# All contractions as pairs of 64-row passes, queries one head at a time inside the attention stream, on fixed bank pairs

## The chip, the cores and the metric

The kernel runs on one core of one Trainium2 chip. The metric is the device time of one execution in microseconds (us); lower is better.

The engines go by short names: PE is TensorE's matmuls and PEld its weight loads, ACT is ScalarE, DVE is VectorE, POOL is GpSimd and SPq is the queue of SyncE. The matmuls write into PSUM, which the program shares out as eight banks.

## The reference, cut to what matters

```python
# x [1,2048,448]; k, v caches [1,8,2048,256]; wq [448,4096]; wo [4096,448]; w_gate, w_up [448,1792]; w_down [1792,448]
xn = layernorm(x)
q  = (xn @ wq)                       # 16 heads of 256, two query heads share one k/v head
s  = softmax(q k^T / 16) v           # over the last 512 keys only
s  = s @ wo
g  = silu((gelu(xn @ w_gate) * (xn @ w_up)) @ w_down)
return x + s * g
```

The contractions are over 448 (queries, gate, up), 256 (scores), 512 (P V), 4096 (w_o) and 1792 (w_down). The rows are worked on in four chunks of 512, so the attention has 4 x 16 = 64 head steps, called "heads" below and numbered 0 to 63.

## The kernel before: the parts that matter

TensorE has 128 rows. A contraction of 448 = 3 x 128 + 64 does not fill it evenly, so the queries and gate/up are already computed as **pairs of 64-row passes**: two matmuls on the upper and the lower half of the rows, side by side, into two different PSUM banks. Phase 0 has the upper rows fill bank b and the lower rows bank b+1; phase 1 has it the other way round, so each bank ends with the full sum. The code makes phase 1 of a bank pair wait until its phase 0 has ended.

```python
def group(units, lo, hi, start, stop, phases=(0, 1)):
    for p in phases:
        ...
        for (b, w, wr, cols, reads, rreads, xts) in units:
            for k in ks:
                for u, j in ((0, ph), (1, 1 - ph)):          # rows 0-63, then rows 64-127
                    rows = slice(R * u, R * u + R)
                    lst.append((bank[b + j][:, lo:hi], l, xnT[rows, k, cols], ...))
            before = [last_row[b][0]] if b in last_row and last_row[b][1] != ph else []
            o = mms(lst, reads + rr + xb, b_ps[b:b + 2], before)
```

The other contractions are full 128-row passes. Queries come in blocks of 8 or 12 heads, then scores and P V alternate for as many heads. P V of a head follows its scores by two heads (LAG = 2), and alternates between two bank pairs (`m % 2 * 2`).

```python
def s_mm(m):                                             # scores of head m: 4 tiles of 128 rows
    for t4 in range(4):
        b = AB[t4]
        mms([(bank[b], qT[:, s, e, t4 * P:(t4 + 1) * P], kT[:, g, e, :], e == 0, e == 1) for e in range(2)], ...)
        # ACT: exp with row sum; DVE: reciprocal, then normalise into pn
        if t4 % 2 == 1:
            dma_t(pT..., pn...)                          # transposed by DMA

def pv(m):
    for e in range(2):
        b = BB[m % 2 * 2 + e]
        mms([(bank[b]..., va[:, g, j, e * P:(e + 1) * P], pT[:, x, :, :, j, :]..., j == 0, j == NJ - 1)
             for j in range(NJ)], ...)
        # e == 0: ACT copies the bank into oT; e == 1: DVE does

for m in range(NS):                                      # NS = 64
    if m in groups:                                      # 0, 8, 20, 32, 44, 56
        for i in range(m, groups[groups.index(m) + 1], 2):
            q_group(i, (cur, nxt)[i // 2 % 2])
    s_mm(m)
    ...
    if len(late) == LAG:
        pv(late.pop(0))
    ...                                                  # after each chunk: w_o, 4 tiles
```

`mms` issues a list of matmuls with one wait ahead and one semaphore at the end. Below, a "slot" is the time of one full pass or of one pair.

The softmax here doesn't subtract the row's maximum and nothing guards it: scores larger than these inputs give would overflow.

Of the kernel before, what the change touches and what calls it, by code (L numbers as in the profile page):

```python
# [164 lines left out]
def bass_recurrent_scan__sliding_block_cached__geglu_ffn__prompt_kernel(  # L165
# [34 lines left out]
    QS = 12  # L200

    es = ExitStack()
    with es:
# [86 lines left out]
        NPT, NPN, NP32 = 3, 3, 3  # L290
        pT, a, at = place("pT", [P, NPT, 2, 2, NJ, P], BF16, at=rf)
        b_pT = [sbuf_bufs(a + i * QC * NJ * 2, QC * NJ, 2) for i in range(NPT)]
# [7 lines left out]
        qT, a, at = place("qT", [P, QS, 2, QC], BF16, at=b_gl[0].lo - (QS - HG) * 2 * QC * 2)  # L300
        assert b_oT[-1].hi <= a
        b_qT = [[K.buf(a + (h * 2 + e) * QC * 2, QC * 2) for e in range(2)] for h in range(QS)]

# [136 lines left out]

        def warm(n, b, w):
            def fn(e):
                ins = None
                for i in range(n):
                    ins = e.matmul(bank[b][:, 0:w], lhsT=gl[:, 0, 0:P], rhs=gl[:, 0, 0:w], start=True, stop=True)
                return ins
            last_row[b] = (K.op("pe", fn, (b_gl[0],), b_ps[b:b + 2]), None)
# [48 lines left out]

        def down(c, pairs):
            for t4 in range(4):
                t = c * 4 + t4
                b = bk(pairs, t4)  # L500
                mms([(bank[b][:, 0:D], actT[:, c % 2, f, t4 * P:(t4 + 1) * P], wd[:, f, :], f == 0, f == NF - 1)
                     for f in range(NF)], [b_wd] + b_actT[c % 2], (b_ps[b],))
                s = t % 2
                act(tmp[:, s, :], bank[b][:, 0:D], ACT.Tanh, (b_ps[b],), b_tmp[s], scale=0.5)
                K.op("dve", lambda e, t=t, b=b, s=s: e.scalar_tensor_tensor(
                    out=g2[:, t, :], in0=tmp[:, s, :], scalar=1.0, in1=bank[b][:, 0:D],
                    op0=ALU.add, op1=ALU.mult), b_tmp[s] + [b_ps[b]], (b_g2[t],))
# [29 lines left out]
        warm(2, 2, QC // 2)  # L537
# [82 lines left out]
        def q_group(n, pairs):  # L620

            c, h = divmod(n, Hq)
            units = [(b, lambda j, k, i=i: wq[:, k, (h + i) * Dh + j * P:(h + i) * Dh + (j + 1) * P],
                      wqr[:, h + i, :], slice(c * QC, (c + 1) * QC), b_wql[h // HG][:1], b_wql[h // HG][1:], b_xnT[c * 4:c * 4 + 4])
                     for i, b in enumerate(pairs)]
            group(units, 0, QC, True, True)
            for i, b in enumerate(pairs):
                s = qs(n + i)
                act(qT[:, s, 0, :], bank[b], ACT.Copy, (b_ps[b],), (b_qT[s][0],))
                K.op("dve", lambda v, s=s, b=b: v.tensor_copy(qT[:, s, 1, :], bank[b + 1]),  # L630
                     (b_ps[b + 1],), (b_qT[s][1],))
# [3 lines left out]
        def s_mm(m):  # L635
            s, g = qs(m), m % Hq // 2
            for t4 in range(4):
                b = AB[t4]
                mms([(bank[b], qT[:, s, e, t4 * P:(t4 + 1) * P], kT[:, g, e, :], e == 0, e == 1) for e in range(2)],
                    [b_kT[g]] + b_qT[s], (b_ps[b],))  # L640
                n = m * 4 + t4
                r, z, y, x = n % NRS, n % NP32, n // 2 % NPN, n // 4 % NPT
                K.op("act", lambda e, b=b, r=r, z=z: e.activation(  # L643
                    p32[:, z, :], bank[b], ACT.Exp, scale=att_scale, accum_out=rsum[:, r:r + 1]),
                    (b_ps[b],), (b_p32[z], b_rsum[r]))
                K.op("dve", lambda e, r=r: e.reciprocal(rden[:, r:r + 1], rsum[:, r:r + 1]), (b_rsum[r],), (b_rden[r],))  # L646
                K.op("dve", lambda e, r=r, z=z, y=y, t=t4 % 2: e.tensor_scalar(  # L647
                    pn[:, y, t, :], p32[:, z, :], rden[:, r:r + 1], None, op0=ALU.mult),
# [145 lines left out]
```

## Time and profile before

| | before |
|---|---|
| time, median of the first 3 runs (range) | 556.31 us (556.21 to 556.72) |
| span in the profile | 554.7 us |
| TensorE busy | 99% of the span |
| chain that ended last | 98% TensorE |
| gate/up stream (first matmul after TensorE's last transposes) from | 10.0 us |
| last matmul starts | 551.1 us |

From the page of the kernel before, part 1 (busy time, share of the span, instructions; PEld is the weight load) and the first line of part 4 (the chain of work that ended last):

```profile
PE 547.6 (99%) x3603; PEld 261.2 (47%) x3628; DVE 317.2 (57%) x817; ACT 273.6 (49%) x727; POOL 32.7 (6%) x64
...
PE 98%; DMA 1%; issue 0%; DVE 0%; SPq 0%; ACT 0%
```

The Trainium skill, "Perfetto Trace Analysis", Identifying the Most-Contended Engine, warns that matmul busy time is no measure of how close TensorE is to its peak, because matmuls are pipelined. That holds here: the profiled duration of one matmul is 379 ns, yet one starts every 216. What tells is the distance from start to start. From the timeline of TensorE before (start, duration, then what ran, with the number of matmuls), a stretch of scores and P V that ends in a query block:

```profile
164.81 1.89 PE L328 MATMUL bank<-kT,qT 128*128 128x512 bf16 x8
166.53 1.89 PE L328 MATMUL bank<-pT,va 128*128 128x512 bf16 x8
168.26 1.89 PE L328 MATMUL bank<-kT,qT 128*128 128x512 bf16 x8
169.99 1.89 PE L328 MATMUL bank<-pT,va 128*128 128x512 bf16 x8
171.81 0.82 PE L328 MATMUL bank<-xnT,wq 64*128 64x512 bf16 x6
172.47 0.38 PE L328 MATMUL bank<-xnT,wqr 64*128 64x512 bf16 x2
```

Eight full matmuls take 166.53 - 164.81 = 1.72 us (1.727 unrounded), 216 ns each. Six 64-row matmuls, three pairs, take 172.47 - 171.81 = 0.66 us: 216 ns a pair, with 10 ns more in all just after the border. The border between them is different: the last P V stretch lasts 171.81 - 169.99 = 1.82 us, 0.1 us over. There TensorE changes from 128-row to 64-row tiling. Such a loss is called a drain below, after the page that the prediction cites. The same at the two borders of w_down:

```profile
36.84 1.48 PE L328 MATMUL bank<-xnT,wgu 64*128 64x512 bf16 x12
38.25 10.77 PE L328 MATMUL bank<-wd,actT 128*128 128x448 bf16 x56
48.95 0.82 PE L328 MATMUL bank<-xnT,wgu 64*128 64x512 bf16 x6
```

Six pairs take 1.41 us in place of 1.30, and 56 matmuls of 448 columns 10.70 in place of 10.59 (189.2 ns each).

### The profile page before, as it was taken

Reading aid. Unit: us, or ns where it says so; the run is one execution under the profiler, and the core shown is the slowest. Engines: PE = TensorE matmul, PEld = TensorE weight load, DVE = VectorE, ACT = ScalarE, POOL = GpSimd, SP = SyncE. Lnnn points to the kernel's source line nnn. Section 1 sums busy time; section 2 is a strip of 40 time slices with the busy share of each in tenths; the row PEclk is TensorE's granted clock in tenths of the full one; section 3 lists DMA queues with packets and bytes.
Section 4 is the critical chain, followed back from the end, with each engine's and each line's share of the span. In section 5 each row is a group of like instructions: output and inputs, shape, how many; then the busy total and the mean of one; then the engine's idle time right before and its main releaser. Section 6 shows DMA issues by size and latency. Waiting matters only on the chain.

```text
span 554.7 us, 9719 instructions
## 1 busy us (share of the span) xinstructions
PE 547.6 (99%) x3603; PEld 261.2 (47%) x3628; DVE 317.2 (57%) x817; ACT 273.6 (49%) x727; POOL 32.7 (6%) x64
## 2 busy tenths in 40 slices
PE   8999999999999999999999999999999999999997
PEld 5554444444544444554444444544444454444455
DVE  6673734443385588326588745258747625858722
ACT  5432324353485588205588635058747505758600
POOL 1120580000000000000000000000000000000000
PEclk9999999999999999999999999999999999999999
DMA  9540399901156077413086803157704713618601
GB/s 295 115 141 9 79 302 307 213 1 39 38 134 96 5 149 157 88 35 92 1 153 152 153 1 77 33 94 164 146 11 95 134 34 90 153 19 153 153 8 34
DMA packets 163599, 57.63 MB, mean 104 GB/s; under 512 B 151456, under 2 KB 160672, under 8 KB 163552
## 3 DMA queue, kind: packets, MB, share of 16 engines
q1 hardware_dynamic: 159488, 45.16, 38.8%
q0 software_dynamic: 3296, 11.27, 6.7%
q8 instruction: 29, 0.48, 0.4%
q10 hardware_dynamic: 768, 0.57, 0.3%
q14 instruction: 18, 0.15, 0.1%
HBM read 17.92 MB, written 1.84 MB: 36 GB/s over the span
## 4 chain that ended last, share of the span: by engine, by line
PE 98%; DMA 1%; issue 0%; DVE 0%; SPq 0%; ACT 0%
PE bank L328 98%; DMA x<-in_A_x_dram 1%; SPq L316 0%; DVE stats L375 0%; ACT xnT L322 0%; DVE tmp L681 0%; ACT ve L391 0%; DVE ofin L684 0%; PE bank L426 0%; DVE mv L378 0%
## 5 line engine op out<-in xcount | busy, mean ns | idle before, releaser
L643 ACT ACTIVATE p<-bank 128x512 f32<-128x512 f32 x256 | 149.2, 597 | 103.3 <-PE bank L328 101.4
L647 DVE TENSOR_SCALAR pn<-p,rden 128x512 bf16<-128x512 f32 x256 | 124.6, 487 | 14.4 <-DMA pT<-pn 5.4
L328 PE MATMUL bank<-pT,va 128*128 128x512 bf16 x512 | 120.8, 379 | 0.0
L328 PE MATMUL bank<-kT,qT 128*128 128x512 bf16 x487 | 117.8, 379 | 2.0 <-ACT qT L322 1.0
L328 PE MATMUL bank<-wo,oT 128*128 128x448 bf16 (+2 forms) x544 | 97.7, 341 | 0.0
L328 PE MATMUL bank<-xnT,wq 64*128 64x512 bf16 x768 | 94.4, 376 | 0.0
L328 PE MATMUL bank<-xnT,wgu 64*128 64x512 bf16 (+2 forms) x768 | 83.9, 350 | 0.4 <-ACT xnT L322 0.4
L328 PEld LDWEIGHTS bank<-pT,va 128*128 128x128 bf16 x512 | 50.1, 98 | 60.4 <-DMA pT<-pn 0.2
L328 PEld LDWEIGHTS bank<-kT,qT 128*128 128x128 bf16 x512 | 49.6, 98 | 61.3 <-issue 2.5
L328 PEld LDWEIGHTS bank<-wo,oT 128*128 128x128 bf16 x544 | 52.0, 98 | 45.5
L630 DVE CAST qT<-bank 128x512 bf16<-128x512 f32 x64 | 42.9, 692 | 51.9 <-PE bank L328 51.9
L322 ACT ACTIVATE qT<-bank 128x512 bf16<-128x512 f32 x64 | 38.2, 597 | 60.7 <-PE bank L328 59.1
L328 PEld LDWEIGHTS bank<-xnT,wq 64*128 64x128 bf16 x768 | 36.9, 94 | 46.5 <-ACT p L643 2.1
L322 ACT ACTIVATE gl<-bank 128x512 bf16<-128x512 f32 x56 | 33.2, 597 | 49.4 <-PE bank L328 46.2
L494 DVE TENSOR_TENSOR actT<-bank,gl 128x512 bf16<-128x512 f32 x56 | 37.8, 689 | 33.4 <-PE bank L328 26.6
L328 PEld LDWEIGHTS bank<-xnT,wgu 64*128 64x128 bf16 x768 | 36.9, 94 | 37.4 <-issue 0.7
L643 ACT ACTIVATION_READ_ACCUMULATOR p<-bank 128x1 f32 x256 | 52.8, 206 | 0.0
L646 DVE RECIPROCAL rden<-rsum 128x1 f32<-128x1 f32 x256 | 40.4, 158 | 20.6 <-ACT p L643 20.0
L681 DVE SCALAR_TENSOR_TENSOR tmp<-bank,g 128x448 f32<-128x448 f32 (+2 forms) x17 | 10.1, 597 | 72.5 <-PE bank L328 72.5
L666 DVE CAST oT<-bank 128x512 bf16<-128x512 f32 x64 | 43.8, 684 | 6.9 <-PE bank L328 6.9
L328 PE MATMUL bank<-wd,actT 128*128 128x448 bf16 x224 | 43.0, 353 | 0.0
L322 ACT ACTIVATE oT<-bank 128x512 bf16<-128x512 f32 x64 | 39.1, 611 | 7.0 <-PE bank L328 7.0
(39 smaller groups left out, 182.9 us busy)
## 6 DMA issues: line engine op xcount, KB each, us to landing
wo<-in_A_wo_dram POOLq DMA_DIRECT2D x4, 896.0 KB, 19.0
wq<-in_A_wq_dram POOLq DMA_DIRECT2D x2, 1536.0 KB, 10.0
va<-in_A_v_cache_dram POOLq DMA_DIRECT2D x8, 256.0 KB, 13.9
pT<-pn SPq DMA_TRANSPOSE x128, 2.8
xr<-in_A_x_dram POOLq DMA_DIRECT2D x16, 112.0 KB, 2.3
out_dram<-ofin SPq DMA_DIRECT2D x15, 112.0 KB, 1.7
wd<-in_B_w_down_dram SPq DMA_DIRECT2D x1, 1568.0 KB, 7.6
x<-in_A_x_dram SPq DMA_DIRECT2D x2, 448.0 KB, 4.4
```

Of the source, the lines that this page charges most:

```text
L322: K.op("act", lambda e, o=o, i=i: e.activation(o, i, func, scale=scale), reads, writes)
L328: ins = e.matmul(o, lhsT=l, rhs=r, start=st, stop=sp)
L494: K.op("dve", lambda e: e.tensor_tensor(actT[:, c % 2, f, :], bank[b + 1], gl[:, s, :], ALU.mult), (b_ps[b + 1], b_gl[s]), (b_actT[c % 2][ ...
L630: K.op("dve", lambda v, s=s, b=b: v.tensor_copy(qT[:, s, 1, :], bank[b + 1]), (b_ps[b + 1],), (b_qT[s][1],))
L643: K.op("act", lambda e, b=b, r=r, z=z: e.activation(p32[:, z, :], bank[b], ACT.Exp, scale=att_scale, accum_out=rsum[:, r:r + 1]), (b_ps[b] ...
L646: K.op("dve", lambda e, r=r: e.reciprocal(rden[:, r:r + 1], rsum[:, r:r + 1]), (b_rsum[r],), (b_rden[r],))
L647: K.op("dve", lambda e, r=r, z=z, y=y, t=t4 % 2: e.tensor_scalar(pn[:, y, t, :], p32[:, z, :], rden[:, r:r + 1], None, op0=ALU.mult), (b_p ...
L666: K.op("dve", lambda v, i=i, b=b: v.tensor_copy(oT[:, i, :], bank[b]), (b_ps[b],), (b_oT[i],))
L681: K.op("dve", lambda e: e.scalar_tensor_tensor(out=tmp[:, s, c0:c1], in0=bank[b][:, c0:c1], scalar=0.5, in1=g2[:, t, c0:c1], op0=ALU.mult, ...
```

## The change

The intent: make everything pairs of 64-row passes, so that TensorE never changes its tiling. Since phase 1 must not stand directly behind its phase 0, the phases of scores, P V and queries are interleaved within a head, which needs one query head per step rather than blocks. The eight banks are shared out for good: four (AB) for scores, one pair (BB[0]) for the queries of head m + 2, one pair (BB[2]) for P V of head m - 3 (LAG = 3).

```diff
+        HV = halves()        # per phase: (rows 0-63, bank v), (rows 64-127, the other bank)
...
+        def q_mm(n, ph):
+            if n < NS:
+                group([q_unit(n, BB[0])], 0, QC, True, True, (ph,))
+                if ph == 1:
+                    q_evac(n, BB[0])
...
-        def pv(m):
+        def pv(m, ph, b=None):
...
+            b = BB[2] if b is None else b
+            o = mms([(bank[b + v]..., va[rows, g, j, v * P:(v + 1) * P], pT[x][rows, :, :, j, :]...,
+                      ph == 0 and j == 0, ph == 1 and j == NJ - 1) for j in range(NJ) for rows, v in HV[ph]],
+                    ..., [first["p", b]] if ph else [])
...
         for m in range(NS):
-            if m in groups:
-                ...
-            s_mm(m)
-            ...
+            p = m - LAG
+            if m > 0:
+                q_mm(m + 2, 0)
+            s_mm(m, 0, 0)
+            if p >= 0:
+                pv(p, 0)
+            else:
+                s_mm(m, 1, 0)
+            if m > 0:
+                q_mm(m + 2, 1)
+            s_mm(m, 0, 1)
+            if p >= 0:
+                s_mm(m, 1, 0)
+                pv(p, 1)
...                                              # after each chunk: w_o in pairs of tiles
+            s_mm(m, 1, 1)
```

`s_mm(m, i, ph)` is phase ph of tiles 2i and 2i+1. After phase 1, ACT and DVE do what they did before. w_down and w_o become pairs too, but the last w_o tiles at the end stay full passes. `q_mm(n, ph)` is phase ph of the queries of head n, if `n < NS`.

More of the change, by code (lines that the diff above doesn't have):

```diff
@@ L199, in bass_recurrent_scan__sliding_block_cached__geglu_ffn__prompt_kernel @@
     NG = Hq // HG
-    QS = 12
+    QS = 4
     es = ExitStack()
@@ L287, in bass_recurrent_scan__sliding_block_cached__geglu_ffn__prompt_kernel, with place_pT @@
         b_gl = sbuf_bufs(a, QC * 2, NGL)
-        NPT, NPN, NP32 = 3, 3, 3
-        pT, a, at = place("pT", [P, NPT, 2, 2, NJ, P], BF16, at=rf)
-        b_pT = [sbuf_bufs(a + i * QC * NJ * 2, QC * NJ, 2) for i in range(NPT)]
+        NPT, NPN, NP32 = 4, 3, 3
+        pT = [None] * NPT
+        b_pT = [None] * NPT
+        at = rf
+        def place_pT(i, at):
+            pT[i], a, at = place("pT%d" % i, [P, 2, 2, NJ, P], BF16, at=at)
+            b_pT[i] = sbuf_bufs(a, QC * NJ, 2)
+            return at
+        for i in range(NPT - 1):
+            at = place_pT(i, at)
         pn, a, at = place("pn", [P, NPN, 2, W], BF16, at=at)
@@ L299, in bass_recurrent_scan__sliding_block_cached__geglu_ffn__prompt_kernel @@
         b_oT = sbuf_bufs(a, QC * 2, NCO)
-        qT, a, at = place("qT", [P, QS, 2, QC], BF16, at=b_gl[0].lo - (QS - HG) * 2 * QC * 2)
-        assert b_oT[-1].hi <= a
+        assert at <= b_gl[0].lo
+        qT, a, at = place("qT", [P, QS, 2, QC], BF16, at=b_gl[0].lo)
         b_qT = [[K.buf(a + (h * 2 + e) * QC * 2, QC * 2) for e in range(2)] for h in range(QS)]
+        at = place_pT(NPT - 1, at)
         pall = [es.enter_context(nc.psum_tensor("bank%d" % i, [P, 1024], F32)) for i in range(4)]
@@ L439, in bass_recurrent_scan__sliding_block_cached__geglu_ffn__prompt_kernel, with warm_pairs, fn @@
         last_row = {}
+        def warm_pairs(n, b, w):
+            def fn(e):
+                ins = None
+                for i in range(n):
+                    for u in range(2):
+                        r = slice(R * u, R * u + R)
+                        ins = e.matmul(bank[b + u][:, 0:w], lhsT=gl[r, 0, 0:P], rhs=gl[r, 0, 0:w], start=True, stop=True)
+                return ins
+            last_row[b] = (K.op("pe", fn, (b_gl[0],), b_ps[b:b + 2], after=[last_row[b][0]]), None)
         def warm(n, b, w):
@@ L495, in gu_evac, with halves @@
                  (b_ps[b + 1], b_gl[s]), (b_actT[c % 2][f],))
+        def halves():
+            return [[(slice(R * u, R * u + R), u ^ ph) for u in range(2)] for ph in range(2)]
+        HV = halves()
         def down(c, pairs):
-            for t4 in range(4):
-                t = c * 4 + t4
-                b = bk(pairs, t4)
-                mms([(bank[b][:, 0:D], actT[:, c % 2, f, t4 * P:(t4 + 1) * P], wd[:, f, :], f == 0, f == NF - 1)
-                     for f in range(NF)], [b_wd] + b_actT[c % 2], (b_ps[b],))
-                s = t % 2
-                act(tmp[:, s, :], bank[b][:, 0:D], ACT.Tanh, (b_ps[b],), b_tmp[s], scale=0.5)
-                K.op("dve", lambda e, t=t, b=b, s=s: e.scalar_tensor_tensor(
-                    out=g2[:, t, :], in0=tmp[:, s, :], scalar=1.0, in1=bank[b][:, 0:D],
-                    op0=ALU.add, op1=ALU.mult), b_tmp[s] + [b_ps[b]], (b_g2[t],))
+            first = [None, None]
+            for ph in range(2):
+                for i in range(2):
+                    b = pairs[i]
+                    o = mms([(bank[b + v][:, 0:D], actT[rows, c % 2, f, (2 * i + v) * P:(2 * i + v + 1) * P],
+                              wd[rows, f, :], ph == 0 and f == 0, ph == 1 and f == NF - 1)
+                             for f in range(NF) for rows, v in HV[ph]],
+                            [b_wd] + b_actT[c % 2], b_ps[b:b + 2], first[i:i + 1] if ph else [])
+                    first[i] = o
+                    for v in range(2 * ph):
+                        t = c * 4 + 2 * i + v
+                        s = t % 2
+                        act(tmp[:, s, :], bank[b + v][:, 0:D], ACT.Tanh, (b_ps[b + v],), b_tmp[s], scale=0.5)
+                        K.op("dve", lambda e, t=t, b=b + v, s=s: e.scalar_tensor_tensor(
+                            out=g2[:, t, :], in0=tmp[:, s, :], scalar=1.0, in1=bank[b][:, 0:D],
+                            op0=ALU.add, op1=ALU.mult), b_tmp[s] + [b_ps[b + v]], (b_g2[t],))
         def ln_first(t):
@@ L536, in bass_recurrent_scan__sliding_block_cached__geglu_ffn__prompt_kernel @@
         ln_tp_pe(0, ((0, 6), (1, 4)))
-        warm(2, 2, QC // 2)
+        warm_pairs(2, 2, QC // 2)
         ln_second(1, "act")
@@ L617, in bass_recurrent_scan__sliding_block_cached__geglu_ffn__prompt_kernel, with q_unit @@
                 cur, nxt = nxt, cur
-        def q_group(n, pairs):
+        def q_unit(n, b):
             c, h = divmod(n, Hq)
-            units = [(b, lambda j, k, i=i: wq[:, k, (h + i) * Dh + j * P:(h + i) * Dh + (j + 1) * P],
-                      wqr[:, h + i, :], slice(c * QC, (c + 1) * QC), b_wql[h // HG][:1], b_wql[h // HG][1:], b_xnT[c * 4:c * 4 + 4])
-                     for i, b in enumerate(pairs)]
-            group(units, 0, QC, True, True)
-            for i, b in enumerate(pairs):
-                s = qs(n + i)
-                act(qT[:, s, 0, :], bank[b], ACT.Copy, (b_ps[b],), (b_qT[s][0],))
-                K.op("dve", lambda v, s=s, b=b: v.tensor_copy(qT[:, s, 1, :], bank[b + 1]),
-                     (b_ps[b + 1],), (b_qT[s][1],))
+            return (b, lambda j, k: wq[:, k, h * Dh + j * P:h * Dh + (j + 1) * P], wqr[:, h, :],
+                    slice(c * QC, (c + 1) * QC), b_wql[h // HG][:1], b_wql[h // HG][1:], b_xnT[c * 4:c * 4 + 4])
@@ L633, in bass_recurrent_scan__sliding_block_cached__geglu_ffn__prompt_kernel, with q_evac, s_mm @@
+        def q_evac(n, b):
+            s = qs(n)
+            act(qT[:, s, 0, :], bank[b], ACT.Copy, (b_ps[b],), (b_qT[s][0],))
+            K.op("dve", lambda v: v.tensor_copy(qT[:, s, 1, :], bank[b + 1]), (b_ps[b + 1],), (b_qT[s][1],))
+        def q_mm(n, ph):
[3 more added lines that the diff above has]
+                    q_evac(n, BB[0])
         AB, BB = [], []
-        def s_mm(m):
+        first = {}
+        def s_mm(m, i, ph):
@@ L636, in s_mm @@
             s, g = qs(m), m % Hq // 2
-            for t4 in range(4):
-                b = AB[t4]
-                mms([(bank[b], qT[:, s, e, t4 * P:(t4 + 1) * P], kT[:, g, e, :], e == 0, e == 1) for e in range(2)],
-                    [b_kT[g]] + b_qT[s], (b_ps[b],))
-                n = m * 4 + t4
-                r, z, y, x = n % NRS, n % NP32, n // 2 % NPN, n // 4 % NPT
-                K.op("act", lambda e, b=b, r=r, z=z: e.activation(
+            b = AB[2 * i]
+            o = mms([(bank[b + v], qT[rows, s, e, (2 * i + v) * P:(2 * i + v + 1) * P], kT[rows, g, e, :],
+                      ph == 0 and e == 0, ph == 1 and e == 1) for e in range(2) for rows, v in HV[ph]],
+                    [b_kT[g]] + b_qT[s], b_ps[b:b + 2], [first["s", i]] if ph else [])
@@ L644, in s_mm @@
+            first["s", i] = o
+            if ph == 0:
+                return
+            y, x = (2 * m + i) % NPN, m % NPT
+            for v in range(2):
+                n = m * 4 + 2 * i + v
+                r, z = n % NRS, n % NP32
+                K.op("act", lambda e, b=b + v, r=r, z=z: e.activation(
                     p32[:, z, :], bank[b], ACT.Exp, scale=att_scale, accum_out=rsum[:, r:r + 1]),
-                    (b_ps[b],), (b_p32[z], b_rsum[r]))
+                    (b_ps[b + v],), (b_p32[z], b_rsum[r]))
@@ L646, in s_mm @@
                 K.op("dve", lambda e, r=r: e.reciprocal(rden[:, r:r + 1], rsum[:, r:r + 1]), (b_rsum[r],), (b_rden[r],))
-                K.op("dve", lambda e, r=r, z=z, y=y, t=t4 % 2: e.tensor_scalar(
-                    pn[:, y, t, :], p32[:, z, :], rden[:, r:r + 1], None, op0=ALU.mult),
+                K.op("dve", lambda e, r=r, z=z, v=v: e.tensor_scalar(
+                    pn[:, y, v, :], p32[:, z, :], rden[:, r:r + 1], None, op0=ALU.mult),
                     (b_p32[z], b_rden[r]), (b_pn[y],))
-                if t4 % 2 == 1:
-                    dma_t(pT[:, x, t4 // 2, :, :, :].rearrange("p t j q -> p (t j) q"),
-                          pn[:, y, :, :].rearrange("p t k -> p (t k)"), (b_pn[y],), (b_pT[x][t4 // 2],))
@@ L654, in pv @@
-        def pv(m):
+            dma_t(pT[x][:, i, :, :, :].rearrange("p t j q -> p (t j) q"),
+                  pn[:, y, :, :].rearrange("p t k -> p (t k)"), (b_pn[y],), (b_pT[x][i],))
+        def pv(m, ph, b=None):
             h = m % Hq
             g, x = h // 2, m % NPT
-            for e in range(2):
-                b = BB[m % 2 * 2 + e]
-                mms([(bank[b].rearrange("p (t q) -> p t q", q=P), va[:, g, j, e * P:(e + 1) * P],
-                      pT[:, x, :, :, j, :].rearrange("p a t q -> p (a t) q"), j == 0, j == NJ - 1)
-                     for j in range(NJ)], [b_va[g]] + b_pT[x], (b_ps[b],))
-                i = 2 * h + e
-                if e == 0:
-                    act(oT[:, i, :], bank[b], ACT.Copy, (b_ps[b],), (b_oT[i],))
-                else:
-                    K.op("dve", lambda v, i=i, b=b: v.tensor_copy(oT[:, i, :], bank[b]), (b_ps[b],), (b_oT[i],))
+            b = BB[2] if b is None else b
+            o = mms([(bank[b + v].rearrange("p (t q) -> p t q", q=P), va[rows, g, j, v * P:(v + 1) * P],
+                      pT[x][rows, :, :, j, :].rearrange("p a t q -> p (a t) q"), ph == 0 and j == 0,
+                      ph == 1 and j == NJ - 1) for j in range(NJ) for rows, v in HV[ph]],
+                    [b_va[g]] + b_pT[x], b_ps[b:b + 2], [first["p", b]] if ph else [])
+            first["p", b] = o
+            if ph == 0:
+                return
+            i = 2 * h
+            act(oT[:, i, :], bank[b], ACT.Copy, (b_ps[b],), (b_oT[i],))
+            K.op("dve", lambda v: v.tensor_copy(oT[:, i + 1, :], bank[b + 1]), (b_ps[b + 1],), (b_oT[i + 1],))
@@ new lines, in wo_reads, with wo_pair @@
+        def wo_reads(ch):
+            return [b_oT[i] for i in ch] + [b_wo[p] for p in sorted({i // 8 for i in ch})]
+        def wo_pair(k, b, ph, lo, hi):
+            ch = list(range(lo, hi))
+            o = mms([(bank[b + v][:, 0:D], oT[rows, i, (2 * k + v) * P:(2 * k + v + 1) * P], wo[rows, i, :],
+                      ph == 0 and i == 0, ph == 1 and i == NCO - 1) for i in ch for rows, v in HV[ph]],
+                    wo_reads(ch), b_ps[b:b + 2], [first["w", k]] if ph else [])
+            if ph == 0:
+                first["w", k] = o
@@ L670, in wo_mm @@
             mms([(bank[b][:, c0:c1], oT[:, i, t4 * P:(t4 + 1) * P], wo[:, i, c0:c1], i == 0, i == NCO - 1)
-                 for i in ch],
-                [b_oT[i] for i in ch] + [b_wo[p] for p in sorted({i // 8 for i in ch})],
-                (b_ps[b],))
-        def wo_fin(c, t4, b, c0=0, c1=D):
-            t = c * 4 + t4
-            s = t % 2
-            hv = [i for i in range(2) if (c0 < CUT, c1 > CUT)[i]]
-            bt = [b_tmp[s][i] for i in hv]
-            bo = [b_ofin[s][i] for i in hv]
-            K.op("dve", lambda e: e.scalar_tensor_tensor(
-                out=tmp[:, s, c0:c1], in0=bank[b][:, c0:c1], scalar=0.5, in1=g2[:, t, c0:c1],
-                op0=ALU.mult, op1=ALU.mult), (b_ps[b], b_g2[t]), bt)
-            K.op("dve", lambda e: e.tensor_tensor(ofin[:, s, c0:c1], tmp[:, s, c0:c1], xr[:, t % NXR, c0:c1], ALU.add),
-                 bt + [b_xr[t % NXR]], bo)
-            dma("sp", out_view[:, t, c0:c1], ofin[:, s, c0:c1], bo, ())
-            if t + NXR < NT:
-                dma("pool", xr[:, t % NXR, :], x_view[:, t + NXR, :], (), (b_xr[t % NXR],))
@@ L690, in bass_recurrent_scan__sliding_block_cached__geglu_ffn__prompt_kernel, with wo_fin @@
-        LAG = 2
-        late = []
+                 for i in ch], wo_reads(ch), (b_ps[b],))
+        added = {}
+        def wo_fin(c, tiles, c0=0, c1=D):
+            hv = [i for i in range(2) if (c0 < CUT, c1 > CUT)[i]]
+            for t4, b in tiles:
+                t = c * 4 + t4
+                s = t % 2
+                K.op("dve", lambda e, t=t, s=s, b=b: e.scalar_tensor_tensor(
+                    out=tmp[:, s, c0:c1], in0=bank[b][:, c0:c1], scalar=0.5, in1=g2[:, t, c0:c1],
+                    op0=ALU.mult, op1=ALU.mult), (b_ps[b], b_g2[t]), [b_tmp[s][i] for i in hv], after=added.pop(s, ()))
+            for t4, b in tiles:
+                t = c * 4 + t4
+                s = t % 2
+                bo = [b_ofin[s][i] for i in hv]
+                added[s] = [K.op("dve", lambda e, t=t, s=s: e.tensor_tensor(
+                    ofin[:, s, c0:c1], tmp[:, s, c0:c1], xr[:, t % NXR, c0:c1], ALU.add),
+                    [b_tmp[s][i] for i in hv] + [b_xr[t % NXR]], bo)]
+                dma("sp", out_view[:, t, c0:c1], ofin[:, s, c0:c1], bo, ())
+                if t + NXR < NT:
+                    dma("pool", xr[:, t % NXR, :], x_view[:, t + NXR, :], (), (b_xr[t % NXR],))
@@ L692, in bass_recurrent_scan__sliding_block_cached__geglu_ffn__prompt_kernel @@
+        LAG = 3
         NS = NQC * Hq
-        groups = [0, HG] + list(range(HG + QS, NS, QS)) + [NS]
         act(tmp[:, 1, 0:1], nhalf[:, :], ACT.Exp, (b_nhalf,), (b_tmp[1][0],))
-        K.reuse([b for y in b_qT[QS - HG:] for b in y])
+        K.reuse([b for y in b_qT for b in y])
         AB.extend(bk(cur, j) for j in range(4))
         BB.extend(bk(nxt, j) for j in range(4))
-        for m in range(NS):
-            if m in groups:
-                for i in range(m, groups[groups.index(m) + 1], 2):
-                    q_group(i, (cur, nxt)[i // 2 % 2])
-                if m == 0:
-                    K.reuse([b for x in b_pT for b in x] + b_pn + b_p32)
-            s_mm(m)
-            if m < LAG:
-                down(NQC - LAG + m, nxt)
-                if m == LAG - 1:
-                    K.reuse(b_oT + [b for y in b_qT[:QS - HG] for b in y])
-            if len(late) == LAG:
-                pv(late.pop(0))
-            if m > Hq and m % Hq == LAG - 1:
-                c = m // Hq - 1
-                for t4 in range(4):
-                    if t4 == 0:
-                        wo_mm(0, BB[0], 0, NCO - 2)
-                        wo_mm(0, BB[0], NCO - 2, NCO)
-                    else:
-                        wo_mm(t4, BB[t4], 0, NCO)
-                    wo_fin(c, t4, BB[t4])
-            late.append(m)
@@ new lines, in bass_recurrent_scan__sliding_block_cached__geglu_ffn__prompt_kernel @@
+        group([q_unit(i, cur[i]) for i in range(2)], 0, QC, True, True)
+        for i in range(2):
+            q_evac(i, cur[i])
+        K.reuse([b for x in b_pT for b in x] + b_pn + b_p32)
+        q_mm(2, 0)
+        q_mm(2, 1)
+        for m in range(NS):
+            p = m - LAG
[12 more added lines that the diff above has]
+                pv(p, 1)
+            if p > 0 and p % Hq == Hq - 1:
+                c = p // Hq
+                wo_pair(0, BB[0], 0, 0, NCO - 2)
+                wo_pair(0, BB[0], 0, NCO - 2, NCO)
+                wo_pair(1, BB[2], 0, 0, NCO)
+                for k in range(2):
+                    wo_pair(k, BB[2 * k], 1, 0, NCO)
+                    wo_fin(c, [(2 * k + v, BB[2 * k + v]) for v in range(2)])
+            s_mm(m, 1, 1)
+            if m < 2:
+                down(NQC - 2 + m, nxt)
+                if m == 1:
+                    K.reuse(b_oT)
@@ L722, in bass_recurrent_scan__sliding_block_cached__geglu_ffn__prompt_kernel @@
+        late = range(NS - LAG, NS)
         c = NQC - 1
         LATE = NCO - 2 * (LAG + 1)
-        wo_mm(0, AB[0], 0, LATE)
-        pv(late.pop(0))
-        pv(late.pop(0))
-        wo_mm(1, AB[1], 0, LATE)
-        wo_mm(0, AB[0], LATE, NCO)
-        wo_fin(c, 0, AB[0])
-        wo_mm(1, AB[1], LATE, NCO)
-        wo_fin(c, 1, AB[1])
-        wo_mm(2, AB[2], 0, NCO)
-        wo_fin(c, 2, AB[2])
+        wo_pair(0, AB[0], 0, 0, LATE)
+        pv(late[0], 0)
+        pv(late[1], 0, BB[0])
+        pv(late[0], 1)
@@ L734, in bass_recurrent_scan__sliding_block_cached__geglu_ffn__prompt_kernel @@
+        pv(late[1], 1, BB[0])
+        wo_pair(0, AB[0], 1, 0, LATE - 4)
+        pv(late[2], 0)
+        wo_pair(0, AB[0], 1, LATE - 4, LATE)
+        pv(late[2], 1)
+        wo_mm(2, AB[2], 0, NCO - 2)
+        wo_mm(2, AB[2], NCO - 2, NCO)
+        wo_fin(c, [(2, AB[2])])
+        for t4 in (1, 0):
+            wo_mm(t4, AB[t4], LATE, NCO)
+            wo_fin(c, [(t4, AB[t4])])
         for i in range(2):
@@ L737, in bass_recurrent_scan__sliding_block_cached__geglu_ffn__prompt_kernel @@
             wo_mm(3, b, 0, NCO, lo, hi)
-            wo_fin(c, 3, b, lo, hi)
+            wo_fin(c, [(3, b)], lo, hi)
         K.schedule()
```

## The prediction

> **What bounds the kernel now.** TensorE. Section 1 of the page has PE busy 99% of a 554.7 us span; the chain that ended last is 98% PE. Busy is not peak for pipelined matmuls, so I read start-to-start times in the timeline: eight full 128-row matmuls of 512 columns take 1.727 us (215.8 ns each) in the score and P V stretches, nine 64-row pairs take 1.943 us (215.8 ns a pair) in the gate/up and query stretches, and 448-column matmuls take 189 ns. A pair of 64-row passes costs exactly what one full pass costs. (The Trainium skill, "TensorE: Matmul & The Clock Gate", Back-to-back issue gap, gives N/2.4 + 2.5 = 215.8 ns; the trace agrees.) Count: (392 gate/up + 448 query + 512 score + 512 P V) x 215.8 + (224 + 512) x 189.2 = 541.5 us. The head takes about 6 us and the tail 3 us. Some 4 us is left to win inside.
>
> **What the change removes.** The drains between 128-row and 64-row tiling (the Trainium skill, "TensorEngine Tiling (Array Packing)", Key Properties: changing the mode drains TensorE; no time given). In the timeline each costs 92 to 107 ns over the ordinary spacing: two into and two out of w_down, six from queries into scores, five from P V to queries: 15, about 1.5 us, all on the critical path. Perhaps 0.2 us more in the head.
>
> **What it adds.** No streaming time: the same slots, twice the PE instructions, which query and gate/up stretches already sustain. One change of tiling in the tail (0.1 us). Phase 1 of a bank pair waits for its phase 0; where they follow directly (head 2's queries, once; nearly so at the first scores) that exposes some 0.3 to 0.5 us, and the first iteration with P V reuses a score bank early, about 0.2 us. Elsewhere 0.86 us or more of other work lies between.
>
> **What it moves.** The attention iteration becomes 23 slots = 4.96 us instead of 3.45 us. ACT needs 4 x 0.57 + 2 x 0.5 = 3.3 us of it, DVE 4 x 0.59 + 2 x 0.56 = 3.5 us: no limit. The tightest loop is the P V bank pair, now one instead of two: DVE's copy of oT stands behind two normalisations. From an iteration's start: query copy on ACT 3.0, exps 3.5 and 4.1, second reciprocal 4.8, normalisation 5.0, copy 5.4 to 6.1; the next P V is due at 6.26. Slack is about 0.1 us. The score banks have over 1 us, the transposes several.
>
> **Prediction: 555.3 us** (before 556.3): -1.5 (drains) +0.7 (start and tail) -0.2 (head). Range 553.8 to 559.0. Faster by over 2%: 0.01; within 2%: 0.95; slower by over 2%: 0.04.
>
> **What would show it.** Start-to-start in the attention stays 215.8 ns a pair, about 4.96 us per head; no gaps near 100 ns at the borders of stretches, bar one in the tail; weight-load instructions about double, their busy share rising towards 80%; PE still 98% of the chain of waits; ACT and DVE slices even out, the eight-tenths slices falling to 6 or 7. If the P V loop is too tight, the waits list PE or PEld waiting for DVE oT, tens of ns to 0.2 us in each of some 60 iterations.
>
> **What would make it wrong.** The oT loop late by 0.1 us every iteration adds 6 us. More semaphore waits on a PE queue that issues an instruction every 54 ns could let the stream slip. Pairs whose moving operand is strided (P V) or whose weights change each pass could run slower than the query pairs measured.

## The result

| | before | after |
|---|---|---|
| time, median (range, 4 runs each) | 556.26 us (556.06 to 556.72) | 556.85 us (556.79 to 556.92) |
| span in the profile | 554.7 us | 555.1 us |
| gate/up stream from | 9.995 us | 9.620 us |
| first query matmul | 114.159 us | 113.339 us |
| last matmul starts | 551.100 us | 551.409 us |

The ratio is 1.0009, 95% interval 0.9992 to 1.0027: the same. (Ratios are the mean time of one kernel's fast runs over that of the other's of the same rounds, so not quite the ratio of the medians quoted.) The change took its 15 drains away and the time did not fall.

The page after, parts 1 and 4:

```profile
PE 548.4 (99%) x5310; PEld 267.3 (48%) x5310; DVE 316.7 (57%) x817; ACT 272.2 (49%) x727; POOL 32.7 (6%) x64
...
PE 97%; DVE 1%; DMA 0%; ACT 0%; issue 0%; DVEq 0%; ACTq 0%
```

The timeline of TensorE around w_down, as above:

```profile
36.47 1.48 PE L337 MATMUL bank<-xnT,wgu 64*128 64x512 bf16 x12
37.76 10.77 PE L337 MATMUL bank<-wd,actT 64*128 64x448 bf16 x112
48.36 0.83 PE L337 MATMUL bank<-xnT,wgu 64*128 64x512 bf16 x6
```

The drains are gone: 1.29 us and 10.60 us. Within an ordinary head of the attention the stream has no gap either:

```profile
183.52 0.59 PE L337 MATMUL bank<-kT,qT 64*128 64x512 bf16 x4
183.95 1.03 PE L337 MATMUL bank<-pT,va 64*128 64x512 bf16 x8
184.82 0.81 PE L337 MATMUL bank<-xnT,wq 64*128 64x512 bf16 x6
```

Two pairs of scores take 0.43 us, four of P V 0.87, a head 4.96 from end to end. But the last two heads are not like that:

```profile
513.00 1.03 PE L337 MATMUL bank<-kT,qT 64*128 64x512 bf16 x8
514.63 1.04 PE L337 MATMUL bank<-pT,va 64*128 64x512 bf16 x8 [0.60 <-DVE oT L710]
515.50 1.03 PE L337 MATMUL bank<-kT,qT 64*128 64x512 bf16 x8
516.37 1.03 PE L337 MATMUL bank<-pT,va 64*128 64x512 bf16 x8
517.23 1.03 PE L337 MATMUL bank<-kT,qT 64*128 64x512 bf16 x8
518.85 1.04 PE L337 MATMUL bank<-pT,va 64*128 64x512 bf16 x8 [0.60 <-DVE oT L710]
```

The score stretches before the two marked lines last 1.63 us in place of 0.86. The bracket names what ended the idle time: the copy of oT by DVE (line 710). At the start of the attention there are smaller losses, for example 1.00 us in place of 0.86 for four pairs of scores:

```profile
146.75 1.03 PE L337 MATMUL bank<-kT,qT 64*128 64x512 bf16 x8
147.75 0.82 PE L337 MATMUL bank<-xnT,wq 64*128 64x512 bf16 x6
```

The whole account, from the start times of the two profiled runs (us, after against before):

| where | difference |
|---|---|
| head, up to the gate/up stream | -0.38 |
| four drains around w_down | -0.45 |
| eleven drains in the attention | about -1.16 |
| start of the attention: query head 2 alone, first use of banks by heads 1 to 3 | +0.65 |
| heads 62 and 63 | +1.54 |
| change back to full passes in the tail | +0.10 |
| after the last matmul | +0.1 |
| **sum** | **+0.4** |

The eleven attention drains are the remainder of that stretch (438.07 us against 436.94), which agrees with the 103 to 107 ns read at each border, the 10 ns at the next matmul included. (25 matmul records are missing in the trace before, so the six borders from queries to scores were read across one missing record; e6's trace lacks none, and its six such borders show 92 to 93 ns and then 10 to 11.) The start is the sum of the excesses over 215.8 or 189.2 ns a pair: 0.25 for head 2's queries, 0.09 + 0.01 ahead of and in w_down, 0.14 + 0.15 + 0.01 around head 3.

### The profile page after: what moved, and what is told of

Its sections match the earlier page's. It is cut to its first block, busy times and chain, and to the rows that moved or that the text cites. A ratio compares the mean times of both kernels' runs of the same rounds, so it can differ in the third digit from the quotient of the medians.

```text
span 555.1 us, 12948 instructions
## 1 busy us (share of the span) xinstructions
PE 548.4 (99%) x5310; PEld 267.3 (48%) x5310; DVE 316.7 (57%) x817; ACT 272.2 (49%) x727; POOL 32.7 (6%) x64
## 4 chain that ended last, share of the span: by engine, by line
PE 97%; DVE 1%; DMA 0%; ACT 0%; issue 0%; DVEq 0%; ACTq 0%
PE bank L337 97%; DMA x<-in_A_x_dram 0%; DVE pn L690 0%; ACT p L686 0%; DVE oT L710 0%; DVE stats L384 0%; PE bank L435 0%; ACT qT L331 0%; DVE rden L689 0%; DVE xn L410 0%; ACT xnT L331 0%; DVE mv L387 0%; DVE tmp L737 0%; DVE ofin L744 0%; DVE rstd L404 0%
## 5 line engine op out<-in xcount | busy, mean ns | idle before, releaser
L337 PE MATMUL bank<-kT,qT 64*128 64x512 bf16 x1024 | 140.9, 376 | 0.0
L337 PE MATMUL bank<-pT,va 64*128 64x512 bf16 x1024 | 131.0, 376 | 1.2 <-DVE oT L710 1.2
L337 PE MATMUL bank<-xnT,wq 64*128 64x512 bf16 x768 | 103.6, 376 | 0.1
L337 PE MATMUL bank<-wo,oT 64*128 64x448 bf16 (+3 forms) x976 | 98.1, 343 | 0.0
L337 PEld LDWEIGHTS bank<-pT,va 64*128 64x128 bf16 x1024 | 49.6, 94 | 62.3 <-DVE oT L710 14.5
L337 PEld LDWEIGHTS bank<-kT,qT 64*128 64x128 bf16 x1024 | 49.8, 94 | 60.7 <-ACT p L686 0.8
L337 PEld LDWEIGHTS bank<-wo,oT 64*128 64x128 bf16 (+1 forms) x976 | 51.7, 94 | 46.0 <-issue 0.4
L659 DVE CAST qT<-bank 128x512 bf16<-128x512 f32 x64 | 44.2, 691 | 41.7 <-PE bank L337 41.7
L337 PEld LDWEIGHTS bank<-xnT,wgu 64*128 64x128 bf16 x768 | 40.7, 94 | 33.1 <-PE bank L337 0.4
L337 PE MATMUL bank<-wd,actT 64*128 64x448 bf16 x448 | 43.1, 349 | 0.0
```

The source lines that it names most:

```text
L337: ins = e.matmul(o, lhsT=l, rhs=r, start=st, stop=sp)
L659: K.op("dve", lambda v: v.tensor_copy(qT[:, s, 1, :], bank[b + 1]), (b_ps[b + 1],), (b_qT[s][1],))
```

## Why the last two heads: the P V loop

My theory (A): after the change P V has one bank pair, so P V of one head must wait until ACT and DVE have copied the previous one out. DVE's copy stands in line behind two normalisations. From the timeline of DVE after, in an ordinary head:

```profile
181.91 0.16 DVE L689 RECIPROCAL rden<-rsum 128x1 f32<-128x1 f32 x1 [0.52 <-ACT p L686]
182.11 0.49 DVE L690 TENSOR_SCALAR pn<-p,rden 128x512 bf16<-128x512 f32 x1
182.51 0.15 DVE L689 RECIPROCAL rden<-rsum 128x1 f32<-128x1 f32 x1
182.70 0.49 DVE L690 TENSOR_SCALAR pn<-p,rden 128x512 bf16<-128x512 f32 x1
183.10 0.68 DVE L710 CAST oT<-bank 128x512 bf16<-128x512 f32 x1
```

and of the weight loads:

```profile
183.31 0.31 PEld L337 LDWEIGHTS bank<-kT,qT 64*128 64x128 bf16 x4
183.84 0.43 PEld L337 LDWEIGHTS bank<-pT,va 64*128 64x128 bf16 x6 [0.22 <-DVE oT L710]
```

The copy ends at 183.10 + 0.68 = 183.78, the weight load for the next P V follows at 183.84, and the P V matmul itself starts at 183.95, which is just when it is due. The load loses half of its usual lead of 0.21 us and the stream loses nothing: a wait that costs no time. In the two stalled heads, where the matmul does start late, the load leads it by only 0.005 us; so of the 0.11 us here about 0.10 are to spare. The list of waits (in total, times, longest) holds both kinds: the two stalls, of up to 1.1 us, are among 57. In e8, the last experiment below, which has no stall there, 55 are left. After the change, then e8:

```profile
PEld bank L337 <- DVE oT L710: 14.5, 57, 1.1
```

```profile
PEld bank L337 <- DVE oT L710: 12.0, 55, 0.2
```

A head without queries (by the condition `n < NS`, heads 62 and 63 have no query head two ahead) is shorter by seven pairs (1.51 us), 3.45 us, but the loop is not shorter by as much: the copy cannot come earlier than the exponentials and normalisations allow. So it is late by 0.76 us, twice.

Rivals: (B) the stalls belong to the end of the program, to score banks or to the tail; a DVE that is busy 57% of the span is no limit. (C) the drains were not worth 0.1 us each, or are paid elsewhere. (D) interleaving the queries was worth something of its own. The expectations name their rivals anew for each run: in e4 it is D that they call B.

## The experiments

All eight gave results within the reference's tolerance. The kernel before, run on the same chips, had medians of 556.30 us (first four) and 556.26 us (last four). There were five runs of each of the first four and of e8, four of e2 and of e3, two of e7. The change itself was not run again; comparisons with its 556.85 us rest on the kernel before, whose medians agree within 0.04 us. By the record's measure of 2% e2 and e7 are slower, e3 is unclear and all the others are the same as before: the small steps rest on the intervals and, above all, on the traces.

| run | edit | expected under A | measured median | ratio to before (95%) |
|---|---|---|---|---|
| e1 | second P V pair in iteration 62 | 555.3 | 555.57 | 0.9984 (0.9971 to 0.9996) |
| e4 | queries in blocks, all pairs | 555 to 557 | 556.00 | 0.9993 (0.9980 to 1.0005) |
| e5 | e1 and start mended | 554.7 to 555.0 | 555.20 | 0.9978 (0.9966 to 0.9991) |
| e6 | before, w_down alone in pairs | 555.9 | 556.05 | 0.9994 (0.9981 to 1.0008) |
| e7 | e4 with one P V pair | 588 | 589.18 | 1.0591 (1.0571 to 1.0610) |
| e2 | P V as full passes | 568.7 | 570.08 | 1.0247 (1.0231 to 1.0263) |
| e3 | one more DVE instruction | 566 | 566.64 | 1.0189 (1.0175 to 1.0203) |
| e8 | e5 mended again | 554.7 | 554.68 | 0.9973 (0.9960 to 0.9985) |

### e1: a second bank pair where the queries have left one free

```diff
+            pb = BB[0] if m == NS - 2 else BB[2]
             if p >= 0:
-                pv(p, 0)
+                pv(p, 0, pb)
...
-                pv(p, 1)
+                pv(p, 1, pb)
```

> The changed kernel with one edit: in the second of the two iterations... precisely, head index 62 (the first of the last two, which have no queries left), P V uses the bank pair that the queries have given up, so the pair is not reused until the iteration after. Theory A (after the change the last two iterations stall because P V must wait for VectorE's copy of oT out of its only bank pair): both stalls of 0.76 us go, the span falls by 1.5 us from 555.1 to about 553.6 and the time to about 555.3. Rival B (they stall because the score banks wait for the exponentials, or because of the tail itself): the stalls stay in place, time 556.8 as the changed kernel.

Measured: 555.57 us, span 553.5. The timeline of TensorE at the place of the stalls:

```profile
512.97 1.03 PE L337 MATMUL bank<-kT,qT 64*128 64x512 bf16 x8
513.83 1.03 PE L337 MATMUL bank<-pT,va 64*128 64x512 bf16 x8
...
516.42 1.03 PE L337 MATMUL bank<-kT,qT 64*128 64x512 bf16 x8
517.29 1.03 PE L337 MATMUL bank<-pT,va 64*128 64x512 bf16 x8
```

0.86 us each: both stalls are gone, and the span is 1.6 us shorter. Rival B would have left them.

### e6: one part of the change alone, four drains

```diff
-                down(DOWN_AT[n + 1], cur)
+                down_pairs(DOWN_AT[n + 1], cur)       # the change's own w_down, in the kernel before
```

> The kernel before with one part of the change alone: w_down of the first two chunks as pairs of 64-row passes, so that four of its 15 changes of tiling vanish. Theory A: each costs about 0.1 us, so the stretch from the first full gate/up group to the first query is 0.4 us shorter and the time about 555.9; too small to be sure of in the times, but plain in the trace. Rival (a drain is hidden, or turns into another wait at the same border): the stretch keeps its length.

Measured: 556.05 us, as expected but, as also expected, not sure in the times. In the trace the stretch from the start of the gate/up stream to the first query is 113.449 - 9.730 = 103.72 us, against 104.16 before: 0.445 us for four drains, 0.11 each. All five pieces of the stretch shrink by just the excess seen before (28.257 to 28.142, 10.700 to 10.593, and so on). In this stretch the drain does not come back as another wait. Later the profiled execution loses 0.25 us of the gain: one P V (at 507.43 us) waits for a DMA transpose (pT), and the kernel before has no such loss there. Whether the edit or chance brought that about is not shown.

### e2: 122 drains put back

```diff
         def pv(m, ph, b=None):
-            o = mms([... for j in range(NJ) for rows, v in HV[ph]], ...)      # four pairs, twice
-            first["p", b] = o
             if ph == 0:
                 return
+            mms([(bank[b + v]..., va[:, g, j, ...], pT[x][:, ...]..., j == 0, j == NJ - 1)
+                 for v in range(2) for j in range(NJ)], ...)                  # eight full passes
```

> The changed kernel with P V alone as full 128-row passes, all eight at the place of its second phase. No streaming time changes (eight slots of 215.8 ns either way), but TensorE changes its tiling twice in each of 61 iterations. Theory A (a change of tiling costs about 0.11 us with its restart; P V later in the iteration takes away the two stalls at the end): 122 x 0.11 = 13.4, less 1.5: 556.85 becomes about 568.7 (566 to 571). Rival (the drains of the kernel before were only seen at the borders of long stretches because other waits met there; inside a stream they hide): about 555.3.

Measured: 570.08 us. From the timeline of TensorE:

```profile
202.15 1.03 PE L337 MATMUL bank<-kT,qT 64*128 64x512 bf16 x8
203.11 1.90 PE L337 MATMUL bank<-pT,va 128*128 128x512 bf16 x8
204.94 0.61 PE L337 MATMUL bank<-kT,qT 64*128 64x512 bf16 x4
205.39 0.81 PE L337 MATMUL bank<-xnT,wq 64*128 64x512 bf16 x6
```

0.96 us for four score pairs in place of 0.86, 1.83 for eight full passes in place of 1.73, and 0.45 in place of 0.43 for the pairs after. A head takes 5.177 us in place of 4.964: 0.107 us for each change of tiling, inside a dense stream too. That leaves nothing of rival C. With two more in the tail, 124 changes of tiling came in, 13.3 us, which is the 13.2 measured, because two old stalls went (1.5 us) and two new ones came (1.5 us). The new ones are the 1.4 us that I missed (the range was 566 to 571): I had expected the stalls of heads 62 and 63 to vanish, but with P V in one piece the scores' two phases stood too close together, and their stretches were 0.74 us too long in each of the two heads, waiting for the first phase and for ACT's exponentials.

### e3: one useless instruction on an engine that is busy 57%

```diff
...                                              # buffers spare and ones, and the filling of ones
             act(oT[:, i, :], bank[b], ACT.Copy, (b_ps[b],), (b_oT[i],))
+            K.op("dve", lambda v: v.tensor_scalar(spare[:, m % 4, :], ones[:, :], epst[:, :], None, op0=ALU.mult), ...)
             K.op("dve", lambda v: v.tensor_copy(oT[:, i + 1, :], bank[b + 1]), ...)
```

> The changed kernel with one useless VectorE instruction (128 x 256, about 0.27 us) ahead of each copy of oT. VectorE is busy 57% of the span. Theory A (the copy ends just 0.1 us before the next P V is due): 0.16 us are added in each of some 59 iterations, and 0.27 us in the last two: about 566 us (561 to 570), with iterations of about 5.12 us. Rival B (a VectorE that is busy 57% hides 0.27 us in an iteration of 4.96 us): 556.9.

Measured: 566.64 us, 9.8 us over the change. The timeline of TensorE:

```profile
205.09 0.59 PE L341 MATMUL bank<-kT,qT 64*128 64x512 bf16 x4
205.68 1.04 PE L341 MATMUL bank<-pT,va 64*128 64x512 bf16 x8
206.55 0.81 PE L341 MATMUL bank<-xnT,wq 64*128 64x512 bf16 x6
```

The two pairs of scores ahead of P V now last 0.59 us in place of 0.43, in every head. A head takes 5.13 us, 0.166 over. I had worked out 0.16 from a slack of 0.1. From the start of the added instruction to the start of the next one on DVE pass 0.262 us, so the slack is 0.262 - 0.166 = 0.10 us. It is real, and DVE's share of busy time says nothing of it.

### e4 and e7: queries in blocks again, with two P V pairs and with one

e4 keeps pairs everywhere, but computes queries in blocks of four heads and lets P V alternate, as the kernel before did:

```diff
+        def q_block(n, bs):
+            for lo in (0, 2):
+                group([q_unit(n + i, bs[i]) for i in (lo, lo + 1)], 0, QC, True, True)
+                ...
-            if m > 0:
-                q_mm(m + 2, 0)
+            if m > 0 and m % 4 == 0:
+                q_block(m, (BB[0], AB[0], BB[2], AB[2]))
+            pb = BB[m % 2 * 2]
...                                              # w_o's two bank pairs change places
-            if m > 0:
-                q_mm(m + 2, 1)
```

> All contractions still as pairs of 64-row passes, but the queries in blocks of four heads ahead of four iterations of scores and P V, as in the kernel before (there 8 and 12), P V alternating between two bank pairs. Theory A (TensorE streams at 215.8 ns a pair whatever the order, so interleaving the queries is worth nothing in itself; only the drains and stalls count): within 1 us of the changed kernel with its last-two-heads stall mended, 555 to 557 us. Rival B (queries between scores and P V relieve ScalarE and VectorE, whose busy tenths reach eight when they stand apart): blocks are slower, by 0.1 us or more in each of 64 iterations, over 562 us.

Measured: 556.00 us, span 554.1. Between the first heads and the last, blocks and heads stream at 215.8 ns a pair without a gap; the version loses 1.1 us once where head 3's scores follow head 2's directly, and 0.15 us at the end. Interleaving is worth nothing in itself (rival D falls), nor is it needed for pairs.

e7 is e4 with the fixed bank pair of the change, and w_o's bank pairs in the order of the change again:

```diff
-            pb = BB[m % 2 * 2]
+            pb = BB[2]
...
-                wb = (BB[2], BB[0])
+                wb = (BB[0], BB[2])
```

> The block version with one edit: P V stays on one fixed bank pair, as in the change, instead of alternating between two. Theory A (with one pair, the loop from P V through the exponentials, the normalisations and VectorE's copy back to P V takes about 4.2 us, which fits into an iteration with queries, 4.96 us, but not into one without, 3.45 us): every iteration that follows another without a query block or an output projection between them, 42 of 64, grows by 0.77 us to 4.23 us; time about 588 us (582 to 592). Rival B (the stalls of the last two iterations belong to the end of the program, where nothing is left to overlap): no stalls, 556 us.

Measured: 589.18 us. The timeline of TensorE and the list of waits (in total, times, longest):

```profile
322.08 1.04 PE L337 MATMUL bank<-pT,va 64*128 64x512 bf16 x8 [0.60 <-DVE oT L710]
322.95 1.03 PE L337 MATMUL bank<-kT,qT 64*128 64x512 bf16 x8
323.82 1.03 PE L337 MATMUL bank<-pT,va 64*128 64x512 bf16 x8
324.68 1.03 PE L337 MATMUL bank<-kT,qT 64*128 64x512 bf16 x8
326.31 1.04 PE L337 MATMUL bank<-pT,va 64*128 64x512 bf16 x8 [0.60 <-DVE oT L710]
```

```profile
PE bank L337 <- DVE oT L710: 24.1, 42, 0.6
```

This head takes 326.31 - 322.08 = 4.23 us, as in the stalled heads after the change (518.85 - 514.63 = 4.22). The stall happens 42 times, the number worked out beforehand, and costs 0.70 to 0.77 us each time, 31 us of the 33 between e7 and e4; most of the rest are three stalls of 0.62 us behind w_o, waiting for DVE's tmp. The stall has nothing to do with the end of the program: it is what one bank pair costs wherever no queries stand between. So fixed bank pairs and interleaving belong together: the interleaving hides the loop that the fixed pairs made.

### e5 and e8: the version that the account points to

e5 has e1's edit, and mends the start. Heads 0 to 2 of the queries form one group; w_down of the last chunk begins on the idle pair; head 4's queries go to the P V pair, not yet in use.

```diff
-        group([q_unit(i, cur[i]) for i in range(2)], 0, QC, True, True)
+        HB = (cur[0], cur[1], BB[0])
+        group([q_unit(i, HB[i]) for i in range(3)], 0, QC, True, True)
...
-        q_mm(2, 0)
-        q_mm(2, 1)
...
+            qb = BB[2] if m == 2 else BB[0]
...
+            if m == 2:
+                s_mm(m, 0, 1)            # ahead of the second query phase
...
-                down(NQC - 2 + m, nxt)
+                down(NQC - 2 + m, (nxt[m], nxt[1 - m]))
```

> The changed kernel with the first edit and the start mended: heads 0, 1 and 2 of the queries as one group of three pairs, so that no phase 1 stands directly behind its phase 0; w_down of the last chunk begins on the idle pair; the queries of head 4 on the P V pair; the third iteration's first scores finished before the second query phase. Theory A (all that the change loses lies at the start, 0.65 us, and in the last two iterations, 1.54 us; the 15 drains, 1.6 us, really are gone): 2.0 to 2.2 us under the changed kernel, span about 553.0, time 554.7 to 555.0, ratio to before 0.997. Rival (the drains were paid elsewhere, for example by the longer chain of semaphores): no better than before, 556.2.

Measured: 555.20 us, 0.2 to 0.5 short of the expectation. Its trace shows why: one gap of 0.50 us ahead of the first P V. By moving head 2's first scores ahead of the query phase I had put two normalisations on DVE ahead of the copy of head 4's queries, and P V needs that bank. The loop's own mistake, made by hand. e8 takes that back, and in head 3 alone does the first P V phase before the first scores:

```diff
-            if m == 2:
-                s_mm(m, 0, 1)
+            if m == 3:
+                s_mm(m, 0, 0)            # behind P V phase 0, not ahead of it
```

> The mended kernel again, because its start still stalls once: the P V of head 0 waits 0.50 us for VectorE's copy of head 4's queries, which stands behind the two normalisations that I had moved ahead of it. Now the third iteration keeps the changed kernel's order and the fourth does its first P V phase before its first scores. Theory A: no gap is left between the first query and the tail; 0.5 us under the mended kernel: span about 552.7, time 554.7, ratio to before 0.997. Rival: the stall moves once more to another wait of the start, and the time stays at 555.2.

Measured: 554.68 us, span 552.8. The timeline of TensorE where the start had stalled:

```profile
147.21 0.83 PE L337 MATMUL bank<-xnT,wq 64*128 64x512 bf16 x6
147.85 0.40 PE L337 MATMUL bank<-xnT,wqr 64*128 64x512 bf16 x2
148.07 1.04 PE L337 MATMUL bank<-pT,va 64*128 64x512 bf16 x8
148.93 0.61 PE L337 MATMUL bank<-kT,qT 64*128 64x512 bf16 x4
```

No gap is left from the first query to the tail. From the start of the gate/up stream to the last matmul e8 takes 539.61 us against 541.11 before: 1.49 us less, the 15 drains less the one in the tail. This version beats both kernels, by 0.27% over the kernel before (0.15 to 0.40%).

## Why the prediction was right or wrong

The measured 556.85 us lies in the range, and "within 2%" was right. The centre was 1.5 us too low, and with it the direction was wrong: 1.0 us less was forecast, 0.6 us more came out, which is the same within the interval. The range reaches from 2.5 us less to 2.7 us more, so it covers both.

- **What bounds the kernel: right.** All streams, full or paired, run at 215.8 ns (512 columns) and 189.2 ns (448 columns) a slot before and after.
- **What the change removes: right.** 1.5 us predicted, about 1.6 measured (0.45 in e6's stretch, about 1.16 in the attention); e2 gives 0.107 us a change of tiling.
- **The P V loop of an ordinary head: right, step by step.** Relative to the start of a head (177.69 in the profile after): query copy 3.01 (predicted 3.0), exponentials 3.51 and 4.08 (3.5 and 4.1), second reciprocal 4.82 (4.8), normalisation 5.01 (5.0), copy 5.41 to 6.09 (5.4 to 6.1), P V at 6.26 (6.26). Slack 0.10 us against "about 0.1".
- **"+0.7 (start and tail)": the term that was mis-sized.** It measured 2.3 us. The start was 0.65 and the change of tiling in the tail 0.10, as foreseen. Missing was 1.54 us for heads 62 and 63. I had worked out the loop for an iteration of 4.96 us and then held it good for all, though the diff's `n < NS` leaves the last two with 3.45 us. e1 took these 1.5 us away, and e7 brought the same stall forth 42 times.
- **"-0.2 (head)": not shown.** The head was 0.38 us shorter in the profiled run, but the changed head's code, the same in eight profiles (after and seven of the experiments; e3 fills one buffer more), reached its gate/up stream anywhere from 9.54 to 10.15 us; e6, with the old head, at 9.73. The timeline of DVE shows the head waiting there for the landing of x.
- **Signs: one wrong, one that told nothing.** The busy share of weight loads was to rise towards 80%, their number to double. The number rose 1.46 times, from 3628 to 5310, because queries and gate/up had been pairs already, and the share went from 47% to 48%: the two loads of a pair mostly start 3 to 4 or some 20 ns apart and their overlap is counted once. (Summed without that, from the durations in the traces, the share rose from 63% to 90%.) And the sign set for too tight a loop, PEld waiting for DVE's oT by up to 0.2 us in some 60 iterations, appeared as listed above, while 55 of those 57 waits cost nothing.

## What to carry to other kernels

When a loop of several engines has just enough slack at the usual iteration length, look for iterations that are shorter, the first and last above all: what the missing work hid is exposed there. Of a wait listed 57 times 55 cost nothing here and two nearly all that the change gained, so judge waits by the start times of the engine that bounds the kernel, not by their totals or by shares of busy time. Here TensorE streamed already, and splitting full passes into row pairs gained only the drains between tilings (15, some 1.6 us); count them before rewriting.

## What the Trainium skill lacked or had wrong

- "TensorEngine Tiling (Array Packing)", Key Properties, says that a change of tiling mode drains TensorE, without a time. The runs show 91 to 97 ns over the ordinary spacing at the change and some 10 ns at the next matmul; 0.107 us a change over a head of e2, 0.111 in e6.
- The same page treats row tiling as a gain for short contractions. No page gives the spacing of a long stream of such pairs, each pass with its own weight load: here it is 215.8 ns a pair at 512 columns, the same as that of a full pass.
- "TensorE: Matmul & The Clock Gate", Back-to-back issue gap, gives 131 ns for sustained matmuls of 512 columns in a stream with weight loads, and 216 ns, the figure that the prediction used, as the isolated gap. Every stream of 512 columns here, each matmul with its own weight load, ran at 215.8 ns, and no two starts a slot apart lie under 214 ns. (Parts 1 and 2 of the page do have 216 ns for back-to-back matmuls.)
- The same page, Part 3, says that weight loads overlap with matmuls in flight only when the row groups differ. In the kernel before, full 128-row weight loads begin 1 to 2 ns after a full 128-row matmul has begun (126.784 and 126.785 us), take 98 ns, and the spacing stays 215.8 ns. (Its Part 2, and the mechanism at the head of Part 3, do speak of a background weight buffer.)
- "Perfetto Trace Analysis", Identifying the Most-Contended Engine, recommends, beside the share of peak FLOPs, the summed time of the weight loads over the window as a measure of how near TensorE is to its peak. Summed so from the traces it was 63% before and 90% after the change, for the same work in the same time, 91% in e8, which has no stalls, and 85% in e7, which has 42: the tiling moved it far more than the stalls did. (With overlapping loads counted once, as on the profile's page, it was 47%, 48%, 54% and 45%.)
